# Threshold attention and a leaky-ReLU MLP on one core: four small moves of work between and along the engines' queues

## The chip, the cores and the metric

The kernel runs on one core of a Trainium2 chip. A core has a matrix engine (TensorE, PE in the profile, with its weight loads as PEld), a vector engine (VectorE, DVE), an activation engine (ScalarE, ACT), a general engine (GpSimd, POOL) and a queue for transfers (SyncE, SP). Each engine works through its own instructions in order, and semaphores hold an instruction until what it needs is there. The metric is the time of one execution on the device in microseconds (us); lower is better.

## The reference

Eight batches of eight heads, 576 tokens, 64 elements a head, then an MLP over the 4608 tokens with 512 inputs and 2048 hidden units:

```
scores = q @ k^T / sqrt(64)
scores = where(scores >= max(scores) - tau, scores, -1e9)      # tau = 0.02
attn   = exp(scores - max(scores));  attn /= sum(attn) + 1e-9
x      = (attn @ v), heads side by side                        # [4608, 512]
h      = x @ w_in;  g = max(0.01 * h, h);  out = g @ w_out
```

All inputs and the output are fp32 in memory.

## The kernel before

The work is cut into 144 steps, 18 for each batch. A step is 128 queries of a pair of heads (h = 0, 1); steps go over two blocks of 256 queries, four pairs p and two halves c, and two more steps a batch take the last 64 queries of all heads ("tail" steps). Two steps c = 0, 1 share one tile of weights. The code is written by hand in the order of a loop over n (lines 482 to 522), and each engine's queue has exactly this order: nothing is scheduled later.

What a step n issues, in this order:

- loads for later batches on SP, `loads_at`
- `exps` of step n-1 on ACT: exp of the scores less their largest. In "steep" steps (all before step 12, later those with no turning in the next step) the second head is done with Prelu and Exp on ACT, which need the threshold; otherwise VectorE masks it
- `scores` of step n on PE (L217): three products of fp16 high and low halves of q and k, into PSUM. There is room for one step's scores, so the next ones wait for the score copy
- `copy_min` on DVE (L225, here called the score copy): scaled and negated scores to SBUF, and their minimum `mn` for each head
- `evacuate` of a PV of the step before: x = PV times the widened 1/sum, on DVE (L326; L316 for tails, tile `xt`)
- the first job of `pool_at` on GpSimd, then `threshold` (L232: `th` = `mn` + tau, on DVE for the first 14 steps and on GpSimd from then on), then the other jobs of `pool_at`: splits of q and k into fp16 halves (L138, L144, L148), casts of v (L107, L112), loads of the MLP's weights (L444, L447)
- for step n-1 `weights` on DVE (L264: mask and sum), `recip` (L270: 1/sum) and `widen` (L273: 1/sum copied 64 times into slot 9 of the weights' tile, on GpSimd). In the first 8 steps ("early") recip and widen come after every step, later once for two steps
- the weights are turned: on PE (`turn_w_pe`, L291, in the step after) for the 8 early steps, with the two halves copied back by ACT and DVE (L293); otherwise by a transposing transfer from SP's queue (`turn_w`, L281). The widened 1/sum is turned with them, which is how it comes to lie along the queries
- one unit of `layer1` (L347, L349), if one is ready; the turning of q and k halves on PE (`turn`, L177, copied back at L180 to L188); two half-units of `layer2` (L360), if there are any
- `pv` (L304) of an earlier pair, 4 steps behind (3 for early steps), into the one PSUM buffer `pv`

A group of 256 tokens is complete when the x of its last pair is formed. It then makes 8 units of layer 1, which may start in the step after the one in which x is issued (`l1q`, with `n + 1`), and then 16 half-units of layer 2. Tail tokens of two batches form a group of 128 with 4 and 8. One unit and two half-units a step are what the loop takes.

Before the loop the first pairs are prepared. `split_now` (L151) makes the halves of a pair on ACT (high half, L158) and DVE (low half, L159). For pair 0's k and q, the tail of k, and pair 1's k and q (`first[0]` to `first[4]`) all halves come before step 0; the next ones are split on GpSimd (`split_pool`).

Of the kernel before, what the change touches and what calls it, by code (L numbers as in the profile page):

```python
# [9 lines left out]
FP32 = mybir.dt.float32  # L10
FP16 = mybir.dt.float16
AX = mybir.AluOpType
AF = mybir.ActivationFunctionType
# [25 lines left out]
def kernel(  # L39
# [10 lines left out]
    nc = tc.nc  # L50
# [4 lines left out]
    tau_f = float(tau)  # L55


    UNIT = 64.0 * 64.0 * 8.0
    sb = ctx.enter_context(tc.tile_pool(name="sb", bufs=1))
# [64 lines left out]
    def pair_of(b, p, which):  # L124
        return raws[b, p // 2, which][:, ds(2 * (p % 2), 2), :].rearrange("p h (t d) -> p h t d", d=64)

    def new_half():
        return sb.tile([128, 2, 4, 2, 64], FP16, tag="half", bufs=4, name="half")
# [22 lines left out]
    def split_now(key):  # L151
        t = halves[key] = new_half()
        for i in range(2):
            if key[1] == "t":
                src, n = tails[key[0], key[2]][:, :, i, :], 2
            else:
                src, n = pair_of(*key)[:, i, :, :], 4
            nc.scalar.activation(out=t[:, 0, 0:n, i, :], in_=src, func=AF.Copy, bias=0.0, scale=64.0)  # L158
            nc.vector.scalar_tensor_tensor(out=t[:, 1, 0:n, i, :], in0=src, scalar=64.0, in1=t[:, 0, 0:n, i, :],  # L159
                                           op0=AX.mult, op1=AX.subtract)  # L160
# [58 lines left out]

    def copy_min(st):  # L220

        st.mn = sb.tile([128, 2], FP32, tag="mn", bufs=3, name="mn")
        st.s = sb.tile([128, 2, 576], FP32, tag="s", bufs=2, name="s")
        for h in range(2):
            nc.vector.tensor_scalar(  # L225
                out=st.s[:, h, :].rearrange("p (a b) -> p a b", a=2), in0=st.sc[h][:, :, 0:288],
                scalar1=-1.0 / UNIT, scalar2=None, op0=AX.mult, op1=AX.min, accum_out=st.mn[:, h : h + 1])

    def threshold(st):
        st.th = sb.tile([128, 2], FP32, tag="th", bufs=3, name="th")  # L230
        eng = nc.vector if st.n < 14 else nc.gpsimd
        eng.tensor_scalar(out=st.th[:, :], in0=st.mn[:, :], scalar1=1.0, scalar2=tau_f, op0=AX.mult, op1=AX.add)  # L232

    def exps(st):

        c = 0 if st.tail else st.c
        if c == 0:
            pairs["now"] = pr = Pair()
            pr.w = sb.tile([128, 2, 10, 128], FP16, tag="w", bufs=3, name="w")
            pr.sum = sb.tile([128, 2, 2], FP32, tag="sum", bufs=3, name="sum")  # L240
            pr.n = 1 if st.tail else 2
        st.pair = pr = pairs["now"]
        flat = pr.w[:, c, :, :].rearrange("q n d -> q (n d)")
        st.w = [flat[:, ds(576 * h, 576)] for h in range(2)]
        st.sum = [pr.sum[:, c, h : h + 1] for h in range(2)]
        st.e = sb.tile([128, 2, 576], FP16, tag="e", bufs=2, name="e")
        for h in range(2):
            if h and st.steep:
                z = st.s[:, h, :]
                nc.scalar.activation(out=z, in_=z, func=AF.Prelu, bias=st.th[:, h : h + 1], scale=-1.0, alpha=1e20)  # L250
                nc.scalar.activation(out=st.w[h], in_=z, func=AF.Exp, bias=minus_tau[:, :], scale=1.0,  # L251
                                     accum_out=st.sum[h])
            else:
                nc.scalar.activation(out=st.e[:, h, :], in_=st.s[:, h, :], func=AF.Exp, bias=st.mn[:, h : h + 1],  # L254
                                     scale=-1.0)

    pairs = {}
# [4 lines left out]
    def weights(st):  # L262
        for h in range(1 if st.steep else 2):
            nc.vector.scalar_tensor_tensor(  # L264
                out=st.w[h], in0=st.s[:, h, :], scalar=st.th[:, h : h + 1], in1=st.e[:, h, :],
                op0=AX.is_le, op1=AX.mult, accum_out=st.sum[h])

    def recip(pr, c, n):
        pr.rec = sb.tile([128, 2, 2], FP32, tag="rec", bufs=2, name="rec")
        nc.vector.reciprocal(out=pr.rec[:, 0:n, :], in_=pr.sum[:, ds(c, n), :])  # L270

    def widen(pr, c, n):
        nc.gpsimd.tensor_copy(out=pr.w[:, ds(c, n), 9, :].rearrange("q c (h d) -> q c h d", h=2),  # L273
                              in_=pr.rec[:, 0:n, :].unsqueeze(3).to_broadcast([128, n, 2, 64]))

    def new_wt(pr):
        pr.wt = sb.tile([128, 2, 10, 128], FP16, tag="wT", bufs=4, name="wT")
# [17 lines left out]
    def pv(st):  # L295
        st.pv = ps.tile([128, 4, 128], FP32, tag="pv", bufs=1, name="pv")
        wt = st.pair.wt
        for u in range(2 if st.tail else 1):
            for i in range(5):
                for h in range(2):  # L300
                    blk = i if h == 0 else 9 - i
                    rhs = wt[:, 0, blk - (blk > 4), ds(64 * u, 64)] if st.tail else wt[:, :, blk - (blk > 4), :]
                    o = st.pv[ds(64 * h, 64), 0, ds(64 * u, 64)] if st.tail else st.pv[ds(64 * h, 64), 0:2, :]
                    nc.tensor.matmul(out=o, lhsT=v16[st.b % 2][:, st.p + u, blk, :], rhs=rhs,  # L304
                                     start=(i == 0), stop=(i == 4), skip_group_check=True)
# [3 lines left out]
    def evacuate(st, n):  # L309
        wt = st.pair.wt  # L310
        if st.tail:
            if (st.b % 2, st.c) == (0, 0):
                groups["t"] = xg = Group(128, (st.b, None))
                xg.x = sb.tile([128, NP, 128], FP16, tag="xt", bufs=2, name="xt")
            xg = groups["t"]
            nc.vector.tensor_tensor(  # L316
                out=xg.x[:, ds(st.p, 2), ds(64 * (st.b % 2), 64)],
                in0=st.pv[:, 0, :].rearrange("d (u q) -> d u q", u=2),
                in1=wt[:, 0, 9, :].rearrange("d (u q) -> d u q", u=2), op=AX.mult)
            done = (st.b % 2, st.c) == (1, 1)  # L320
        else:
            if st.p == 0:
                groups["m"] = xg = Group(256, (st.b, 2 * st.blk))
                xg.x = sb.tile([128, NP, 256], FP16, tag="x", bufs=3, name="x")
            xg = groups["m"]
            nc.vector.tensor_tensor(out=xg.x[:, st.p, :].rearrange("d (c q) -> d c q", c=2), in0=st.pv[:, 0:2, :],  # L326
                                    in1=wt[:, :, 9, :], op=AX.mult)
            done = st.p == NP - 1
        if done:
            nu = 8 if xg.tokens == 256 else 4  # L330
            l1q.extend((xg, u, nu, n + 1) for u in range(nu))
# [55 lines left out]
    def units(b):  # L387
        u = [(b, p, w_) for p in range(NP) for w_ in "kq"]
        return u[:2] + [(b, "t", "k")] + u[2:] + [(b, "t", "q")]
# [68 lines left out]
    first = units(0)  # L458
# [2 lines left out]
    turn(first[0])  # L461
    turn(first[1], nc.vector.tensor_copy)
    turn(first[2])
    for key in first[3:5]:
        split_now(key)
    for key in first[5:7]:
        split_pool(key)
    for i in range(4):
# [11 lines left out]
    pv_at = {s.n + PV_LAG - s.early: s for s in steps if s.tail or s.c == 1}  # L480
    n = 0
    while n < N + PV_LAG + 2 or l1q or l2q or stores:
        for f in loads_at.get(n, []):
            f()
        if 1 <= n <= N:
            exps(steps[n - 1])
        if n < N:
            scores(steps[n])
            copy_min(steps[n])
        if n - 1 in pv_at:  # L490
            evacuate(pv_at[n - 1], n)
        todo = pool_at.get(n, [])
        for f in todo[:1]:
            f()
        if n < N:
            threshold(steps[n])
        for f in todo[1:]:
            f()
        if 1 <= n <= N:
            last = steps[n - 1]  # L500
            weights(last)
            if last.early:
                recip(last.pair, last.c, 1)
                widen(last.pair, last.c, 1)
            elif last.tail or last.c == 1:
                recip(last.pair, 0, last.pair.n)
                widen(last.pair, 0, last.pair.n)
                turn_w(last.pair)
        while stores:
            store()  # L510
        if l1q and l1q[0][3] <= n:
            layer1()
        for f in turns_at.get(n, []):
            f()
        if 2 <= n < N + 2 and steps[n - 2].early:
            turn_w_pe(steps[n - 2].pair, steps[n - 2].c)
        for _ in range(2):
            if l2q:
                layer2()
        if n in pv_at:  # L520
            pv(pv_at[n])
        n += 1
# [1 line left out]
_INS = ['q', 'k', 'v', 'tau', 'moe_w_in', 'moe_w_out']  # L524
# [31 lines left out]
```

## Time and profile before

| what | value |
|---|---|
| three runs | 520.55, 522.68, 523.26 us; median 522.68 |
| profiled execution | 523.44 us, of which its span is 521.7 us |
| PE busy | 485.7 us, 93% of the span |
| VectorE busy | 422.7 us, 81% |
| ACT busy | 431.9 us, 83% |
| POOL busy | 331.5 us, 64% |
| chain that ended last | PE 65%, DVE 16%, DMA 7%, ACT 6%, POOL 3% |

The profile is of one execution. Its span begins with the first instruction; what lies around it is the difference of 1.7 us. A share of busy time is a mean over stages with different limits, so the stages are looked at one by one. In a listing of instructions each line has the start, the duration, the engine, the line of the kernel, the operation, the tile written and the tiles read; a bracket at the end gives the idle time of the engine just before and what ended it. Lines of the chain have a start, a duration, and the work that the end of the program hung on at that time.

### The profile page before, as it was taken

What the parts mean: (1) busy time and instruction counts of PE and PEld (TensorE: products, weight loads), DVE (VectorE), ACT (ScalarE), POOL (GpSimd) and SP (SyncE); (2) the same over time, 40 slices, a digit from 0 to 9 for tenths busy, and PEclk for the clock granted to TensorE, in tenths of its full rate; (3) what the DMA queues carried; (4) which work ended last, traced back from release to release, by engine and by line L of the source; (5) the groups of instructions that cost most, each with busy time, mean ns of one, the idle gap of its engine ahead of it and who ended that gap; (6) DMA issues with size and microseconds to landing.
All of it is one profiled execution on the core that took longest, in us unless ns stands there. A gap on an engine that the chain in (4) does not pass through costs nothing.

```text
span 521.7 us, 19307 instructions
## 1 busy us (share of the span) xinstructions
PE 485.7 (93%) x7904; PEld 342.0 (66%) x7904; DVE 422.7 (81%) x1200; ACT 431.9 (83%) x733; POOL 331.5 (64%) x545
## 2 busy tenths in 40 slices
PE   5777887999999999999999999999999999999996
PEld 3454665667767766677666766667666766667773
DVE  4899998999999878988899888988899888888100
ACT  5699896998988978998889888998889889999541
POOL 4956699787777767677667777687667872222000
PEclk9899899999999999999999999999999999999999
DMA  8992975989968998889979988879969975757611
GB/s 244 249 230 48 175 171 112 177 193 203 230 116 172 200 204 177 168 152 231 191 146 182 194 199 188 163 155 233 186 149 184 195 158 135 127 102 151 134 43 62
DMA packets 220697, 87.76 MB, mean 168 GB/s; under 512 B 190912, under 2 KB 217536, under 8 KB 220608
## 3 DMA queue, kind: packets, MB, share of 16 engines
q1 hardware_dynamic: 217648, 82.07, 75.3%
q0 software_dynamic: 2688, 4.19, 4.4%
q8 instruction: 62, 1.02, 0.8%
q14 instruction: 27, 0.22, 0.1%
q10 hardware_dynamic: 272, 0.26, 0.1%
HBM read 36.70 MB, written 9.44 MB: 88 GB/s over the span
## 4 chain that ended last, share of the span: by engine, by line
PE 65%; DVE 16%; DMA 7%; ACT 6%; POOL 3%; issue 2%; DVEq 0%; POOLq 0%
PE hp L347 20%; PE o L360 18%; PE sc L217 17%; DVE s L225 8%; DMA wT<-w 7%; PE pv L304 6%; DVE w L264 5%; PE tp L177 4%; ACT e L254 1%; ACT s L250 1%; DVE x L326 1%; ACT kT L188 1%; DMA raw<-in_k_dram 1%; POOL half L148 1%; ACT osb L366 1%
## 5 line engine op out<-in xcount | busy, mean ns | idle before, releaser
L225 DVE TENSOR_SCALAR_CACHE_REDUCE s<-sc 128x576 f32<-128x576 f32 x288 | 205.2, 750 | 46.0 <-PE sc L217 40.5
L264 DVE SCALAR_TENSOR_TENSOR w<-s,th,e 128x576 f16<-128x576 f32 x210 | 177.2, 866 | 1.9 <-DMA wT<-w 1.7
L254 ACT ACTIVATE e<-s,mn 128x576 f16<-128x576 f32 x210 | 155.7, 774 | 1.5 <-DVE s L225 1.3
L360 PE MATMUL o<-wout,g 128*64 128x512 f16 x1152 | 147.5, 379 | 0.7 <-ACT osb L366 0.7
L217 PE MATMUL sc<-kT,qT 64*128 64x288 f16 (+1 forms) x1920 | 139.8, 290 | 7.8 <-DVE s L225 7.5
L347 PEld LDWEIGHTS <-win 128*64 128x64 f16 x2560 | 118.4, 110 | 33.0 <-issue 30.7
L347 PE MATMUL hp<-x,win 128*64 128x256 f16 x2048 | 136.8, 277 | 0.0
L349 ACT ACTIVATE g<-hp 128x512 f16<-128x512 f32 x144 | 85.1, 591 | 58.8 <-PE hp L347 58.2
L217 PEld LDWEIGHTS <-qT 64*128 64x128 f16 (+1 forms) x1920 | 78.6, 98 | 61.4 <-issue 46.4
L232 POOL TENSOR_SCALAR th<-mn 128x2 f32<-128x2 f32 x130 | 54.9, 422 | 84.4 <-DVE s L225 56.6
L360 PEld LDWEIGHTS <-g 128*64 128x64 f16 x1152 | 62.1, 110 | 31.3 <-issue 1.5
L148 POOL TENSOR_TENSOR half<-scaled,half 128x512 f16<-128x512 f32 (+1 forms) x75 | 81.5, 1087 | 1.7
L144 POOL CAST half<-scaled 128x512 f16<-128x512 f32 (+1 forms) x75 | 62.5, 834 | 4.8 <-POOL th L232 0.2
L273 POOL CAST w<-rec 128x256 f16<-128x256 f32 (+1 forms) x84 | 32.0, 381 | 52.2 <-DVE rec L270 50.0
L304 PE MATMUL pv<-wT,v 128*64 128x256 f16 (+1 forms) x960 | 54.1, 248 | 9.8 <-DMA wT<-w 5.2
L250 ACT ACTIVATE s<-s,th 128x576 f32<-128x576 f32 x78 | 60.3, 773 | 3.4 <-POOL th L232 1.9
L251 ACT ACTIVATE w<-s,minus_tau 128x576 f16<-128x576 f32 x78 | 60.5, 775 | 2.8
L304 PEld LDWEIGHTS <-v 128*64 128x64 f16 x960 | 40.8, 111 | 29.9 <-DMA wT<-w 11.5
L177 PE MATMUL tp<-ident,half 128*64 128x128 f16 x1152 | 49.3, 229 | 7.6 <-ACT half L158 5.2
L138 POOL TENSOR_SCALAR scaled<-raw 128x512 f32<-128x512 f32 x60 | 48.3, 805 | 7.8 <-DMA raw<-in_k_dram 5.9
L177 PEld LDWEIGHTS <-half 128*64 128x64 f16 x1152 | 42.3, 116 | 11.8 <-ACT half L158 5.9
L188 ACT COPY kT<-tp 128x1024 f16<-128x1024 f16 x32 | 32.3, 1008 | 5.6 <-PE tp L177 5.6
(39 smaller groups left out, 278.8 us busy)
## 6 DMA issues: line engine op xcount, KB each, us to landing
vraw<-in_v_dram SPq DMA_DIRECT2D x16, 512.0 KB, 5.1
out_dram<-osb SPq DMA_DIRECT2D x16, 512.0 KB, 3.4
raw<-in_k_dram SPq DMA_DIRECT2D x14, 512.0 KB, 4.7
raw<-in_q_dram SPq DMA_DIRECT2D x14, 512.0 KB, 4.8
win<-in_moe_w_in_dram POOLq DMA_DIRECT2D x4, 512.0 KB, 10.9
wout<-in_moe_w_out_dram POOLq DMA_DIRECT2D x4, 512.0 KB, 9.1
wT<-w SPq DMA_TRANSPOSE x76, 5.2
raw<-in_k_dram SPq DMA_DIRECT2D x4, 256.0 KB, 4.3
```

The lines of the kernel that those rows point to most:

```text
L144: nc.gpsimd.tensor_copy(out=halves[key][:, 0, 0:n, :, :], in_=scaled[key][:, 0:n, :, :])
L148: nc.gpsimd.tensor_tensor(out=halves[key][:, 1, 0:n, :, :], in0=scaled.pop(key)[:, 0:n, :, :], in1=halves[key][:, 0, 0:n, :, :], op=AX.sub ...
L177: nc.tensor.transpose(o, half[:, x, t, h, :], ident[:, :])
L217: nc.tensor.matmul(out=o, lhsT=lhs, rhs=turned[st.b, "k"][rows, kx, pair, ds(key0, 288)], start=(i == 0), stop=(i == 2), skip_group_check= ...
L225: nc.vector.tensor_scalar(out=st.s[:, h, :].rearrange("p (a b) -> p a b", a=2), in0=st.sc[h][:, :, 0:288], scalar1=-1.0 / UNIT, scalar2=No ...
L250: nc.scalar.activation(out=z, in_=z, func=AF.Prelu, bias=st.th[:, h : h + 1], scale=-1.0, alpha=1e20)
L254: nc.scalar.activation(out=st.e[:, h, :], in_=st.s[:, h, :], func=AF.Exp, bias=st.mn[:, h : h + 1], scale=-1.0)
L264: nc.vector.scalar_tensor_tensor(out=st.w[h], in0=st.s[:, h, :], scalar=st.th[:, h : h + 1], in1=st.e[:, h, :], op0=AX.is_le, op1=AX.mult, ...
L304: nc.tensor.matmul(out=o, lhsT=v16[st.b % 2][:, st.p + u, blk, :], rhs=rhs, start=(i == 0), stop=(i == 4), skip_group_check=True)
L347: nc.tensor.matmul(out=hp[ds(64 * u2, 64), jj, :], lhsT=w_in16[:, i, ds(128 * j + 64 * u2, 64)], rhs=g.x[:, i, :], start=(i == 0), stop=(i ...
L349: nc.scalar.activation(out=g.g[:, ds(nj * u, nj), :], in_=hp[:, :, :], func=AF.Prelu, bias=0.0, scale=1.0, alpha=0.01)
L360: nc.tensor.matmul(out=g.o[ds(64 * u2, 64), :], lhsT=g.g[:, j, ds(128 * m + 64 * u2, 64)], rhs=w_out16[:, j, :], start=(j == 0), stop=(j = ...
```

## The change

Four edits:

- `mn` and `th` become [128, 2, 2] in place of [128, 2], and only the first element of each pair is used: the two thresholds of a step lie 8 bytes apart. The instructions are the same.
- `widen` takes an engine, and the 8 early steps give it VectorE. The later ones stay on GpSimd.
- The split of pair 1's q (`first[4]`) is issued in step 0 after the first score copy, no longer before the loop. On DVE its two instructions now stand behind the two of the score copy; the order on ACT and PE stays.
- `evacuate` is called straight after `pv` at the end of the same step, no longer in the next step behind the score copy. On DVE x moves ahead of the next step's score copy. A group becomes ready for layer 1 one step earlier: its first unit is issued in step 11 where it was step 12, and the stores on SP follow a step earlier too.

```diff
     def copy_min(st):
-        st.mn = sb.tile([128, 2], FP32, tag="mn", bufs=3, name="mn")
+        st.mn = sb.tile([128, 2, 2], FP32, tag="mn", bufs=3, name="mn")
...
-                scalar1=-1.0 / UNIT, scalar2=None, op0=AX.mult, op1=AX.min, accum_out=st.mn[:, h : h + 1])
+                scalar1=-1.0 / UNIT, scalar2=None, op0=AX.mult, op1=AX.min, accum_out=st.mn[:, h, 0:1])

     def threshold(st):
-        st.th = sb.tile([128, 2], FP32, tag="th", bufs=3, name="th")
+        st.th = sb.tile([128, 2, 2], FP32, tag="th", bufs=3, name="th")
         eng = nc.vector if st.n < 14 else nc.gpsimd
-        eng.tensor_scalar(out=st.th[:, :], in0=st.mn[:, :], scalar1=1.0, scalar2=tau_f, op0=AX.mult, op1=AX.add)
+        eng.tensor_scalar(out=st.th[:, :, 0], in0=st.mn[:, :, 0], scalar1=1.0, scalar2=tau_f, op0=AX.mult, op1=AX.add)
...
-    def widen(pr, c, n):
-        nc.gpsimd.tensor_copy(out=pr.w[:, ds(c, n), 9, :].rearrange("q c (h d) -> q c h d", h=2),
-                              in_=pr.rec[:, 0:n, :].unsqueeze(3).to_broadcast([128, n, 2, 64]))
+    def widen(pr, c, n, eng=None):
+        (eng or nc.gpsimd).tensor_copy(out=pr.w[:, ds(c, n), 9, :].rearrange("q c (h d) -> q c h d", h=2),
+                                     in_=pr.rec[:, 0:n, :].unsqueeze(3).to_broadcast([128, n, 2, 64]))
...
-    for key in first[3:5]:
-        split_now(key)
+    split_now(first[3])
...
             copy_min(steps[n])
-        if n - 1 in pv_at:
-            evacuate(pv_at[n - 1], n)
+        if n == 0:
+            split_now(first[4])
...
             if last.early:
                 recip(last.pair, last.c, 1)
-                widen(last.pair, last.c, 1)
+                widen(last.pair, last.c, 1, nc.vector)
...
         if n in pv_at:
             pv(pv_at[n])
+            evacuate(pv_at[n], n)
```

More of the change, by code (lines that the diff above doesn't have):

```diff
@@ L249, in exps @@
                 z = st.s[:, h, :]
-                nc.scalar.activation(out=z, in_=z, func=AF.Prelu, bias=st.th[:, h : h + 1], scale=-1.0, alpha=1e20)
+                nc.scalar.activation(out=z, in_=z, func=AF.Prelu, bias=st.th[:, h, 0:1], scale=-1.0, alpha=1e20)
                 nc.scalar.activation(out=st.w[h], in_=z, func=AF.Exp, bias=minus_tau[:, :], scale=1.0,
@@ L253, in exps @@
             else:
-                nc.scalar.activation(out=st.e[:, h, :], in_=st.s[:, h, :], func=AF.Exp, bias=st.mn[:, h : h + 1],
+                nc.scalar.activation(out=st.e[:, h, :], in_=st.s[:, h, :], func=AF.Exp, bias=st.mn[:, h, 0:1],
                                      scale=-1.0)
@@ L264, in weights @@
             nc.vector.scalar_tensor_tensor(
-                out=st.w[h], in0=st.s[:, h, :], scalar=st.th[:, h : h + 1], in1=st.e[:, h, :],
+                out=st.w[h], in0=st.s[:, h, :], scalar=st.th[:, h, 0:1], in1=st.e[:, h, :],
                 op0=AX.is_le, op1=AX.mult, accum_out=st.sum[h])
```

## The prediction

> **What bounds the kernel now.** I read four views in this order: the windows, the waits by engine, the chain of the first 100 us, and the order of time around single steps. First the windows: core time, then busy time of PE, PEld, DVE, ACT and POOL, and the granted clock.
>
> ```profile
> 13.00:26.00 13.00, 9.58 (x122) 6.35 (x123) 10.55 (x28) 9.01 (x16) 12.57 (x20) 0.84 1.11 250
> 39.00:52.00 13.00, 9.13 (x151) 6.16 (x152) 12.54 (x39) 11.86 (x19) 8.65 (x15) 1.00 0.30 50
> 300.00:350.00 50.00, 49.41 (x802) 34.59 (x800) 43.85 (x126) 43.81 (x75) 37.36 (x61) 1.00 0.85 178
> 500.00:510.00 10.00, 10.00 (x204) 7.91 (x201) 0.00 (x0) 4.78 (x8) 0.00 (x0) 1.00 0.14 54
> ```
>
> There are three stages. Up to about 65 us PE is idle for a quarter of the time; from 39 to 52 DVE is busy for 12.54 of 13 us and sets the pace. From 91 to 480 PE is the bound (382.1 of 389.0 us busy). From 480 PE alone finishes the MLP. So a gain on DVE counts only early, and later only what makes PE wait.
>
> The chain of the early part (start, duration, what):
>
> ```profile
> 17.82 1.68 POOL half L148
> 19.50 0.60 POOL scaled L138
> ...
> 20.85 1.67 POOL half L148
> 22.52 0.24 POOL w L273
> 22.77 0.04 issue
> 22.81 0.32 PE wp L291
> ...
> 36.55 0.57 DVE th L232
> 37.12 0.49 DVE w L264 x2
> ```
>
> POOL's splits stand in front of the first widening (L273), and PE's turn of the first weights waits for it; from 31 to 64 the chain is nearly all DVE. What the threshold on DVE waits for is seen by laying POOL beside DVE:
>
> ```profile
> 36.35 0.81 POOL L447 DMA_DIRECT2D wout<-in_moe_w_out_dram  x1
> ```
>
> ```profile
> 36.55 0.57 DVE L232 TENSOR_SCALAR th<-mn 128x2 f32<-128x2 f32 x1
> ```
>
> The threshold takes 0.16 when POOL rests (33.59). Here it ends at 37.12, as POOL's instruction ends (37.16); at 39.89 it ends with POOL's subtraction (40.42). The 14 on DVE average 0.356, so 0.20 of waiting each, at most 0.46.
>
> A steady stretch, PE and then DVE:
>
> ```profile
> 259.85 0.51 PE L304 MATMUL pv<-wT,v 128*64 128x64 f16 x20
> ...
> 263.41 0.51 PE L304 MATMUL pv<-wT,v 128*64 128x64 f16 x20 [0.36 <-DVE xt L316]
> ```
>
> ```profile
> 258.01 0.76 DVE L225 TENSOR_SCALAR_CACHE_REDUCE s<-sc 128x576 f32<-128x576 f32 x1 [0.94 <-PE sc L217]
> ...
> 259.37 0.42 DVE L326 TENSOR_TENSOR x<-pv,wT 128x256 f16<-128x256 f32 x1
> ...
> 263.07 0.28 DVE L316 TENSOR_TENSOR xt<-pv,wT 128x128 f16<-128x128 f32 x1
> ```
>
> DVE stands idle before the score copy of just the step that follows a PV, and x comes only after that copy. Where two PVs follow each other, PE waits for xt, as PV has one PSUM buffer.
>
> The last stage, one loop turn from start to start:
>
> ```profile
> 497.82 1.05 PE L347 MATMUL hp<-x,win 128*64 128x256 f16 x16
> 498.69 1.04 PE L360 MATMUL o<-wout,g 128*64 128x512 f16 x8
> 499.56 1.05 PE L347 MATMUL hp<-x,win 128*64 128x256 f16 x16
> ```
>
> **x at the end of PV's step.** No instruction is added. DVE runs x ahead of the next score copy, POOL's thresholds and SP's order are kept, except that stores come a step earlier. It adds a wait of DVE for PV; behind it stands the score copy, whose scores come behind the same PV on PE anyway. PV ends 0.84 before those scores, and x takes 0.42, so it fits where DVE is idle (52 waits for scores, 38.0 us, between 91 and 480: median near 0.7).
>
> *Tail.* A group becomes ready for layer 1 one step earlier (step 11, not 12). Following the queues through, 130 layer-1 units and 246 half-units of layer 2 stand before the last scores, not 129 and 244: one turn of 1.74 us leaves the end. It goes into step 11 and step 18, where PE is not the bound: in step 11 it was idle 1.00 + 0.40 us for DVE, and a unit takes 0.99 (1.85 at the low clock that 54.06 shows). Bounds there: 1.6 better (the clock stays up through 52.5 to 56) to 0.5 worse; I take 0, as the idle of 1.38 at 62.30 was followed by full speed. **-1.74.**
>
> *Waits of PE.* Five waits for xt (0.36 to 0.39) go: -1.83. The wait of 1.17 for x at 84.01 goes, but the score copy behind x then ends 0.35 later than it did, so -0.55. x no longer stands between the score copy and the weights, so the weights are 0.34 earlier; of PE's waits for the transposed weights (191.06, 249.93, 308.80, 368.01, 427.29: 1.22 to 0.24) that helps where SP was free, three times some 0.3: -0.9. Where DVE is late (115.43), the score copy now comes up to 0.34 later, and a group's first layer-1 unit can wait 0.1 for x: +0.4, bounds 0 and 1.7 (five such). **-2.9.**
>
> **The first 8 widenings on DVE.** POOL loses eight of 0.29; DVE gains eight. Each must await its reciprocal, so about 0.3 (reciprocal 0.17, of which 0.10 was already counted, and 128 elements, between the 0.17 of the reciprocal and the 0.29 of POOL's). It is one source, SBUF to SBUF, like the threshold, so I add the threshold's mean wait of 0.20; c = 0.5, bounds 0.2 (no wait, short) and 2.0 (all of the longest POOL instruction, 1.68).
>
> **Pair 1's q split behind the first score copy.** DVE's first score copy moves from 12.99 to about 11.6, its exp on ACT from 13.78 to 13.3 (the kT copy stands before it). But PE's transposes of that q wait for its low halves, now behind the copy (1.4), and the scores of step 1 stand behind them: ready at 14.4, done at 15.0 instead of waiting for DVE till 14.47. Step 1 is 0.7 later.
>
> **The opening, walked.** With free thresholds and widenings at no cost: score copy 1 at 16.7 (was 15.89), weights 0 at 18.3, turned weights no longer wait the 2.98 till 22.81; now DVE is late next: copy 2 ends 20.8, weights, reciprocal, q copy 0.6 and wT copy 0.4 follow, copy 3 starts at 23.0 (was 24.71), copy 4 at 26.1 (28.33), x and copy 5 end at 31.3 (33.6). Lead 2.3, q's 0.7 included. From there DVE is the chain. Eight widenings cost 8 x 0.5 = 4.0, all on DVE's path.
>
> **Strided thresholds.** The seven that waited sat at 14.46, 17.37, 20.17 (1.07 over 0.17 together, within the walk) and 36.55, 39.89, 52.74, 58.61 (1.56). No row shows a strided pair. Bounds: no wait (-1.56, and the walk stands) or as before (+1.07 on the walk). The DVE row of the same size that never waits is the reciprocal (0.17, 24 times, beside the same POOL work), so the form decides, not the size; a strided pair is another form, and I take no wait. On POOL, from step 14, nothing changes.
>
> Opening: -2.3 + 4.0 - 1.56 = **+0.1**. Sum: 0.1 - 2.9 - 1.74 = -4.5. The profiled execution (523.44, span 521.7) is 0.76 above the median; from it 518.9, from the median of 522.68 **518.2**.
>
> The Trainium skill, "SBUF — State Buffer", Who interferes with whom, says that VectorE in a two-port mode and GpSimd exclude each other for whole instructions; the two ends above agree. Its "Vector Engine (DVE) Microarchitecture Reference", 5.1, asks for SBUF operands and an even outermost dimension, and for no unit step: by that the strided pair would wait as before, and the sum be rival B's.
>
> **The rivals.**
> - A, neither waits: stepped operands keep both the strided threshold and the widening (its source repeats) clear of POOL, c = 0.3. Opening -2.3 + 2.4 - 1.56 = -1.5; 516.6. For it: the reciprocal's rows. Against: the widening writes densely.
> - B, the stride does nothing: opening -2.3 + 1.07 + 4.0 = +2.8; sum -1.9, 520.8. For it: stride or not, the same two elements move.
> - C, slower: x delays the score copy. Place: 91 to 480, each second step, price 0.34 where DVE comes late; all 64 would be 21.8. It cancels the gain of 4.5 at 13 exposed steps, and is 0.5% slower at 21: with 30, 522.7 + 5.7 = 528.4. Against it: DVE idles in 52 of some 58 such steps.
> - D, the widening meets POOL's long subtractions (1.09 mean): c near 1.0 gives opening +4.1, 522.2. POOL is busy 71% of 13 to 65, but mostly with shorter instructions.
>
> **How the numbers follow.** Forecast 0.35, A 0.24, B 0.23, C 0.08, D 0.10. 0.5% is 2.6 us, about what can be told from no change. The forecast, A and a third of B lie under 520.1: 0.66; the rest of B and D within: 0.25; C above 525.3 and a little else: 0.09. The range goes from A with the kept clock and no late copies (516.6 - 1.6 - 0.4 = 514.6) to D with all five late copies (522.2 + 1.3 = 523.5); C is left out.
>
> **What would show it.** Right: x directly before the score copy, no PE wait for xt, 1.74 less after the last PV; no PE wait for the widening near 20; thresholds at 0.17. Wrong: DVE thresholds still ending with POOL's instructions (B), widenings of 1 us (D), more waits of scores for score copies past 91 (C). A copy 5 ending later than 33.6 would break the walk.

## The result, and the profile after

| | before | after |
|---|---|---|
| runs | 520.55 to 524.66 us, median 522.97 (4 runs) | 516.40 to 517.84 us, median 517.16 (4 runs) |
| profiled execution (span) | 523.44 us (521.7) | 517.33 us (515.6) |
| PE / VectorE / ACT / POOL busy | 485.7 / 422.7 / 431.9 / 331.5 us | 482.9 / 432.6 / 431.8 / 339.8 us |

The ratio is 0.9892, 95% interval 0.985 to 0.9934: faster by 1.1%. A second set of runs of the same kernel gave 517.15 us and 0.9877 (0.9852 to 0.9903).

To see where the time went I laid the two executions beside each other by steps, taking the start of each step's score copy (L225), and cut them into three stretches:

| stretch | before | after | difference | forecast |
|---|---|---|---|---|
| start to the score copy of step 48 | 172.00 | 173.75 | +1.75 | -0.44 |
| step 48 to step 143 (the last) | 308.28 | 301.56 | -6.72 | -2.34 |
| step 143 to the end of the span | 41.4 | 40.3 | -1.1 | -1.74 |
| span | 521.7 | 515.6 | -6.1 | -4.5 |

(In the forecast column the terms of the prediction are put where they act: the opening's +0.1, the wait at 144.82, the one at 84.01 and the late copies in the first row; four waits for xt and the transposed weights in the second.) The sum came near; each of its three parts did not. The first row compares two single executions, and the granted clock differs between them: the kernel before had PE at 0.50 from 21.8 to 28.6 us and from 52.5 to 55.9, the change only from 63.5 to 66.9. Each execution kept here shows one to four such stretches of some 3.4 us between 21 and 126 us, at other places each time.

The middle stretch in the windows of the kernel before (core time, then busy time of PE, PEld, DVE, ACT, POOL, the granted clock, DMA share, GB/s):

```profile
172.00:480.28 308.28, 303.38 (x5012) 212.02 (x5014) 266.34 (x766) 271.75 (x464) 199.89 (x332) 1.00 0.85 175
```

and of the changed kernel:

```profile
173.75:475.31 301.56, 301.36 (x4994) 213.43 (x4996) 271.91 (x766) 271.85 (x464) 209.26 (x333) 1.00 0.89 177
```

PE's idle time there falls from 4.90 us to 0.20: no wait of PE of any size is left there. The waits that are gone, in the waits of PE of the kernel before between 140 and 480 us (us in total, times, longest):

```profile
PE pv L304 <- DMA wT<-w: 1.9, 3, 1.2
PE pv L304 <- DVE xt L316: 1.8, 5, 0.4
PE pv L304 <- DVE w L264: 1.6, 2, 0.8
```

In the changed kernel this view is empty. From step 48 on these are four waits for xt (1.44) and, once a batch, the wait for the transposed weights of its fourteenth step (second block, third pair; 191.06 to 427.29: 1.22 + 0.44 + 0.24 + 0.79 + 0.76 = 3.45), together 4.89. The other 2.02 us of the 6.72 lie in PE's busy time: 16 matmuls less in the stretch up to step 60 (0.46), and 1.56 without any other work gone. Successive groups of matmuls overlap in the records (a layer-1 unit of 1.06 us starts its successor after 0.90), and at a wait this overlap of 0.16 is missing; nine waits make 1.4. By that a wait of PE cost about its idle time and 0.16 more. This is an accounting from the records; no run isolates it. Nor is all of the 6.72 the change's: the run of one-element thresholds alone, further down, has the same code as the kernel before from step 14 on, and its middle stretch took 306.69 us, 1.59 less, with waits for transposed weights of 2.2 us in place of 3.45. Nine executions of kernels with x moved and nothing held back lie between 301.1 and 301.7. So by these profiles the gain there is 5.0 to 7.1 us.

A batch's tail steps in the changed kernel, PE and then DVE:

```profile
259.19 0.48 PE L304 MATMUL pv<-wT,v 128*64 128x64 f16 x20
...
260.44 1.06 PE L347 MATMUL hp<-x,win 128*64 128x256 f16 x16
261.34 1.03 PE L360 MATMUL o<-wout,g 128*64 128x512 f16 x8
262.20 0.48 PE L304 MATMUL pv<-wT,v 128*64 128x64 f16 x20
```

```profile
256.48 0.42 DVE L326 TENSOR_TENSOR x<-pv,wT 128x256 f16<-128x256 f32 x1 [0.23 <-PE pv L304]
257.39 0.76 DVE L225 TENSOR_SCALAR_CACHE_REDUCE s<-sc 128x576 f32<-128x576 f32 x1 [0.49 <-PE sc L217]
...
260.44 0.28 DVE L316 TENSOR_TENSOR xt<-pv,wT 128x128 f16<-128x128 f32 x1
260.63 0.75 DVE L225 TENSOR_SCALAR_CACHE_REDUCE s<-sc 128x576 f32<-128x576 f32 x1
```

x now sits in the idle time ahead of the score copy, which still waits 0.49 for its scores after it, and the second PV finds its buffer free.

The opening is another matter. The first thresholds of the changed kernel on DVE, and what POOL did beside them:

```profile
18.50 0.53 DVE L232 TENSOR_SCALAR th<-mn 128x2 f32<-128x2 f32 x1
...
53.37 0.50 DVE L232 TENSOR_SCALAR th<-mn 128x2 f32<-128x2 f32 x1
...
58.77 0.81 DVE L232 TENSOR_SCALAR th<-mn 128x2 f32<-128x2 f32 x1
```

```profile
17.84 1.15 POOL L148 TENSOR_TENSOR half<-scaled,half 128x512 f16<-128x512 f32 x1
...
53.23 0.62 POOL L138 TENSOR_SCALAR scaled<-raw 128x512 f32<-128x512 f32 x1
...
58.39 1.16 POOL L148 TENSOR_TENSOR half<-scaled,half 128x512 f16<-128x512 f32 x1
```

Each long one ends with POOL's instruction (19.03 and 18.99, 53.87 and 53.85, 59.58 and 59.55). The stride takes no wait away: six of the 14 thresholds still take 0.23 to 0.81. In all they take 4.40 us, before 4.99; POOL did other work beside them, and the run of dense thresholds below separates the two. The widenings on DVE:

```profile
L273 DVE CAST w<-rec x8: 226/233/440, 20.5 to 45.1; 128x128 f16<-128x128 f32 x8
```

(min, median and max in ns.) Two of the eight took 0.44 and 0.30 and ended within 0.09 of the end of a POOL instruction, the others took 0.23 to 0.24. From the start of the reciprocal to the start of what follows the widening it is 3.06 us for the eight; less the prediction's 0.10 for each reciprocal (0.08 to 0.10 before), the eight add 2.26 us to DVE, 0.28 each.

The q split behind the first copy shows on PE in the changed kernel:

```profile
11.79 1.06 PE L177 MATMUL tp<-ident,half 128*64 128x128 f16 x15 [0.33 <-DVE half L159]
14.46 0.97 PE L177 MATMUL tp<-ident,half 128*64 128x128 f16 x8 [1.61 <-DVE half L159]
```

Score copy 0 is 1.33 earlier (11.66), score copy 1 is 1.13 later (17.02 for 15.89), score copy 2 is 1.97 later. PE's wait of 2.98 for the widening at 22.81 is gone, and score copy 3 is back at the time before (-0.07). There the opening stays: copy 5 starts 0.39 later, although PE ran at half its clock in steps 3 and 4 of the kernel before and not in those of the change.

### The profile page after: what moved, and what is told of

Its sections match the earlier page's. It is cut to its first block, busy times and chain, and to the rows that moved or that the text cites. A ratio compares the mean times of both kernels' runs of the same rounds, so it can differ in the third digit from the quotient of the medians.

```text
span 515.6 us, 19350 instructions
## 1 busy us (share of the span) xinstructions
PE 482.9 (94%) x7904; PEld 343.9 (67%) x7904; DVE 432.6 (84%) x1208; ACT 431.8 (84%) x733; POOL 339.8 (66%) x537
## 4 chain that ended last, share of the span: by engine, by line
PE 72%; DVE 12%; DMA 6%; ACT 6%; issue 2%; POOL 1%; SPq 0%; DVEq 0%; POOLq 0%; ACTq 0%
PE hp L347 22%; PE o L360 21%; PE sc L217 18%; PE pv L304 6%; DMA wT<-w 6%; DVE s L225 5%; PE tp L177 4%; DVE w L264 4%; ACT e L254 2%; ACT s L250 1%; DMA rawt<-in_k_dram 1%; ACT w L251 1%; ACT g L349 1%; DVE th L232 1%; DVE wT L293 1%
## 5 line engine op out<-in xcount | busy, mean ns | idle before, releaser
L225 DVE TENSOR_SCALAR_CACHE_REDUCE s<-sc 128x576 f32<-128x576 f32 x288 | 206.1, 753 | 27.5 <-PE sc L217 24.8
L264 DVE SCALAR_TENSOR_TENSOR w<-s,th,e 128x576 f16<-128x576 f32 x210 | 178.9, 875 | 1.1 <-POOL th L232 0.8
L232 POOL TENSOR_SCALAR th<-mn 128x2 f32<-128x2 f32 x130 | 80.8, 622 | 88.1 <-DVE s L225 63.9
L304 PEld LDWEIGHTS <-v 128*64 128x64 f16 x960 | 43.2, 111 | 19.6 <-issue 5.3
L144 POOL CAST half<-scaled 128x512 f16<-128x512 f32 (+1 forms) x75 | 50.7, 676 | 7.6 <-PE tp L177 3.0
L273 POOL CAST w<-rec 128x256 f16<-128x256 f32 (+1 forms) x76 | 29.1, 383 | 30.9 <-DVE rec L270 28.7
```

Of the source, the lines that this page charges most:

```text
L225: nc.vector.tensor_scalar(out=st.s[:, h, :].rearrange("p (a b) -> p a b", a=2), in0=st.sc[h][:, :, 0:288], scalar1=-1.0 / UNIT, scalar2=No ...
L232: eng.tensor_scalar(out=st.th[:, :, 0], in0=st.mn[:, :, 0], scalar1=1.0, scalar2=tau_f, op0=AX.mult, op1=AX.add)
L264: nc.vector.scalar_tensor_tensor(out=st.w[h], in0=st.s[:, h, :], scalar=st.th[:, h, 0:1], in1=st.e[:, h, :], op0=AX.is_le, op1=AX.mult, ac ...
```

## The experiments

All times are medians of four to twelve executions, of which one gave the profile; the kernel before ran on the same chip. Its medians were 523.23 us for the first four runs, 523.52 for the next four and 523.25 for the last four. A ratio's interval is about plus or minus 0.0027, so two of these kernels are told apart from some 2 us on; where a difference is smaller I say what the traces show. The granted clock goes with the times: of the runs of x alone the fastest had a mean of 0.995 (516.28 us), the slowest 0.982 (518.93), by which I estimate 0.2 us for each 0.001. The means of two kernels differ by up to 0.006 (without x last), so differences near 1 us can be the clock's.

### The parts of the change

**x alone.** The kernel before, with x formed at the end of PV's step:

```diff
-        if n - 1 in pv_at:
-            evacuate(pv_at[n - 1], n)
...
             pv(pv_at[n])
+            evacuate(pv_at[n], n)
```

> Only x is moved to the end of PV's step; the three edits of the opening are left as before. Theory 1 (the gain is x's: the PE waits for xt and for the transposed weights once a batch, and one loop turn at the end; the three opening edits together bring nothing): 516 to 518 us, step 143's score copy 4 to 6 us earlier than before. Theory 2 (the sum on record: x's own steps bring 4.6, the opening nothing net): 518.3. Rival (the opening edits bring a third or more of the gain): above 519.

517.72 us, ratio 0.989 (0.9862 to 0.9918). This is the whole of the change's gain within what can be told: step 48 to 143 takes 301.63 us (301.56 in the change), the end is 1.29 shorter.

**Dense thresholds.** The change with its thresholds dense again:

```diff
-        st.th = sb.tile([128, 2, 2], FP32, tag="th", bufs=3, name="th")
+        st.th = sb.tile([128, 2], FP32, tag="th", bufs=3, name="th")
...
-        eng.tensor_scalar(out=st.th[:, :, 0], in0=st.mn[:, :, 0], scalar1=1.0, scalar2=tau_f, op0=AX.mult, op1=AX.add)
+        eng.tensor_scalar(out=st.th[:, :], in0=st.mn[:, :], scalar1=1.0, scalar2=tau_f, op0=AX.mult, op1=AX.add)
```

> The changed kernel with the thresholds dense again ([128, 2]), all else kept. Theory 1 (a strided threshold waits for POOL as a dense one does; the waits became rarer because POOL no longer waits for the widening and runs ahead): within 0.5 us of the changed kernel, the 14 thresholds on DVE again between 0.17 and 0.8 us, each long one ending with an instruction of POOL. The forecast's step (the stride takes the wait away): 1.6 to 2.6 us slower than the changed kernel, with long thresholds where the changed kernel has short ones.

517.12 us, ratio 0.9876 (0.9849 to 0.9902), and the thresholds in order of time are those of the strided kernel, 0.3 us earlier:

```profile
53.05 0.50 DVE L232 TENSOR_SCALAR th<-mn 128x2 f32<-128x2 f32 x1
...
58.45 0.81 DVE L232 TENSOR_SCALAR th<-mn 128x2 f32<-128x2 f32 x1
```

All 14 take 4.39 us, with the stride 4.40. The stride does nothing to the wait.

**Widenings back on GpSimd**, the rest of the change kept:

```diff
-                widen(last.pair, last.c, 1, nc.vector)
+                widen(last.pair, last.c, 1)
```

> The changed kernel with the first 8 widenings on GpSimd again. Theory 1: PE waits again about 3 us for the first widening near 20 us, DVE is spared 8 x 0.28 = 2.3 us, POOL is chained to DVE again; score copy 9 within 1 us of the changed kernel's, total within 1 us. Rival (the widening's move is what helps the opening): 2 us slower or more.

516.78 us, ratio 0.9867 (0.9841 to 0.9894): not to be told from the change. PE's wait for POOL's widening is back, and costs nothing that can be told in the end:

```profile
23.08 0.32 PE L291 MATMUL wp<-ident,w 128*64 128x128 f16 x2 [2.85 <-POOL w L273]
```

**q split before the first copy**, the rest of the change kept:

```diff
-    split_now(first[3])
+    for key in first[3:5]:
+        split_now(key)
...
-        if n == 0:
-            split_now(first[4])
```

> The changed kernel with pair 1's q split ahead of the first score copy again. Theory 1 (the split behind the copy only delays PE's turn of that q and with it the scores of step 1): score copy 1 starts 0.7 to 1.1 us earlier than in the changed kernel, total 0 to 1 us faster. Rival (the earlier first copy and its exp are worth something): slower by 0.5 us or more.

517.11 us, ratio 0.9874 (0.9846 to 0.9901): the change's time to 0.1 us, though score copy 1 is 2.2 us earlier than in the change. In its trace PV waits 4.4 us for transposed weights before 84 us (in the change about 1.0; two more waits of 1.1 follow at 96 and 134): much of the lead of the first steps is given back there.

**The change once more**, nothing edited, for the opening:

> The changed kernel itself once more, on the same chip as the three others, for what two profiles of one program differ by in the first 170 us. Score copy 36 came 2.3 us later than before in its first profile, and 0.3 later with x alone. Theory 1 (the opening edits bring nothing, and the difference is the arrival of transfers): within 1 us of x alone in time, and a score copy 36 between 0 and 2.3 us later than before.

517.15 us, ratio 0.9877 (0.9852 to 0.9903). Score copy 36 starts 2.03 later than in the kernel before and score copy 48 2.14 (2.30 and 1.75 in the first profile): in both of its profiles the opening is behind that of the one profile of the kernel before.

### Why moving x brings so much

**Layer 1 late.** x moved, but layer 1 may start only where it did:

```diff
-            l1q.extend((xg, u, nu, n + 1) for u in range(nu))
+            l1q.extend((xg, u, nu, n + 2) for u in range(nu))
...
-        if n - 1 in pv_at:
-            evacuate(pv_at[n - 1], n)
...
             pv(pv_at[n])
+            evacuate(pv_at[n], n)
```

> Only x moved, as in the run of x alone, but a group's layer 1 may start one step later, so in the same step as before the change. It tells the loop turn at the end from the waits of PE. Theory 1 (two separate gains): the steps from 172 us on pull ahead as with x alone, about 1.1 to 1.3 us a batch, but the end is one turn (1.74 us) longer: 1.0 to 1.8 us slower than x alone, 518.7 to 519.5 us, and no PE wait of layer 1 for x. Rival (the earlier layer 1 is itself what takes the waits away): the waits of PV for the transposed weights stay, 521 us or more.

519.07 us, ratio 0.9929 (0.9905 to 0.9953). Its middle stretch takes 304.11 us, 4.2 less than before where x alone has 6.65 less, and the waits of PE between 140 and 480 us are

```profile
PE pv L304 <- DMA wT<-w: 2.3, 3, 1.4
```

So x's own place removes the waits for xt. That it shortens those for transposed weights is not shown: 2.3 us are left of 3.45, but one-element thresholds alone, with x unmoved, has 2.2. They go away together with the earlier layer 1: in nine executions that have it, with the stores as they follow from it, 0.4 us or less is left from step 48 on. The time is that of theory 1, the reason is in part the rival's.

What follows an earlier layer 1 on SP is that the stores of finished groups come earlier. SP's queue in the kernel before, up to the transfer that the wait at 191.06 is for, the last line:

```profile
171.98 0.58 SPq L375 DMA_DIRECT2D out_dram<-osb  x1
...
175.29 4.95 SPq L281 DMA_TRANSPOSE wT<-w  x1
...
181.59 1.60 SPq L93 DMA_DIRECT2D vraw<-in_v_dram  x1
183.30 4.18 SPq L281 DMA_TRANSPOSE wT<-w  x1
```

and in x alone, where the store went out at 166.85:

```profile
176.15 3.41 SPq L281 DMA_TRANSPOSE wT<-w  x1
...
182.68 4.11 SPq L281 DMA_TRANSPOSE wT<-w  x1
```

The kernel with the late layer 1 has the store where the kernel before has it (170.14, and 4.97 for the first of the two transfers). In the kernel before the queue is in use until 183.19, so the awaited transfer starts 0.93 after its weights are complete (182.37); in x alone it starts 0.03 after (182.65), and PV waits 0.15 in place of 1.22. That is one batch of five. In the other four the awaited transfer of the kernel before starts 0.02 to 0.35 after its weights, and PV waits 0.24 to 0.79. The weights themselves may count too: from the start of their score copy they take 7.6 us before and 7.3 with x moved. And in the kernel with the late layer 1 the transfer of the first batch shown starts 1.06 after its weights, and PV does not wait for it at all. So neither the store nor the weights is shown to be the cause alone.

**x last.** The kernel before with x behind the weights, the reciprocal and the issue of the transposes, to take x out of the weights' way without moving layer 1:

```diff
-        if n - 1 in pv_at:
-            evacuate(pv_at[n - 1], n)
...
+        if n - 1 in pv_at:
+            evacuate(pv_at[n - 1], n)
```

> The kernel before with x put behind the weights, the reciprocal and the issue of the transposing transfer of its step, so later than before. The weights come 0.34 us earlier as in the change, but x and xt come about 1.5 to 2 us later. Theory 1 (PV's waits for the transposed weights went because the weights are earlier): PE's waits for the transfer between 140 and 480 us shrink to under 1.5 us from 3.5 (five), while its waits for xt grow from 0.36 to 1.5 or more each: 523 to 530 us in all. Rival (it is the early x, not the early weights, that ends those waits): PE's waits for the transfer stay at 3 us or more.

540.67 us, ratio 1.033 (1.0302 to 1.0358): far slower than either theory had it. As PV has one buffer, x itself is now late; the waits of PE between 140 and 480 us:

```profile
PE pv L304 <- DVE x L326: 10.0, 6, 2.2
PE pv L304 <- DVE xt L316: 3.7, 6, 0.6
PE pv L304 <- DMA wT<-w: 1.9, 4, 0.9
```

On the transposed weights it decides nothing (1.9 us lies between the two bounds), since PV's times are others here; it shows the price of the opposite move.

**Stores late.** x moved and layer 1 early, but each store is held back one turn of the loop:

```diff
-                stores.append(g)
+                held.append(g)
...
+        stores.extend(held)
+        held.clear()
```

(with x moved as above)

> x at the end of PV's own step, as in the run of that part alone, but each store of an output group is issued one loop turn later, the turn in which the kernel before issues it. Theory (moving x moves the stores, and so takes them from ahead of the transposing transfers of the tail steps on SP; that is why PV's waits for DMA go): between 140 and 480 us PV waits again some 2 us for DMA-transposed weights, and the time is 1 to 2.5 us above the 517.7 of x alone (518.7 to 520). Rival (the stores' place does not matter, layer 1's earlier place or x's own place does it): no DMA wait of PV in that stretch, and within 0.5 us of x alone (517.2 to 518.2).

519.18 us, ratio 0.9919 (0.9888 to 0.995): inside the theory's 518.7 to 520, 1.46 above x alone, which is within the two intervals. Its profiled run is the fastest of its six (517.18); in it the middle stretch takes 303.11 us, 1.5 more than x alone, and PV waits again, but for less than the 2 us expected:

```profile
PE pv L304 <- DMA wT<-w: 1.1, 3, 0.5
```

So the stores' place seems to make a part of these waits: 303.11 us lies outside the 301.1 to 301.7 of the nine executions with early stores. That is one execution, and where PV waits for transfers one and the same code has differed by 1.59 us, so the size, 1.5 of the 2.5 us that the earlier layer 1 brings in this stretch, is not settled; the medians point the same way and do not separate it. What makes the other 1.0 (of which 0.46 are the 16 matmuls) is left open.

### What would have freed the thresholds

**One element at a time.** x moved, and each of the first 14 thresholds as two instructions of one element:

```diff
-        eng.tensor_scalar(out=st.th[:, :], in0=st.mn[:, :], scalar1=1.0, scalar2=tau_f, op0=AX.mult, op1=AX.add)
+        for h in range(2):
+            if st.n < 14:
+                nc.vector.tensor_scalar(out=st.th[:, h : h + 1], in0=st.mn[:, h : h + 1], scalar1=1.0, scalar2=tau_f,
+                                        op0=AX.mult, op1=AX.add)
+            elif h == 0:
+                nc.gpsimd.tensor_scalar(out=st.th[:, :], in0=st.mn[:, :], scalar1=1.0, scalar2=tau_f, op0=AX.mult, op1=AX.add)
```

> Only x moved, and each threshold of the first 14 steps on DVE split into two instructions of one element each. If what makes a threshold wait for POOL is that it is read and written in two halves at once, an instruction of one element has no second half and never waits: 28 thresholds of 0.17 us or less, the sum of waits 2.1 us gone, 14 more instructions at about 0.08; score copy 14 1 to 1.5 us earlier than with x alone, total 0 to 1.5 us faster. If any such instruction waits for POOL: still up to 0.8 us each.

514.89 us, ratio 0.9839 (0.9813 to 0.9865), 2.8 us below x alone and more than the 0 to 1.5 expected; the intervals just touch. None of the 28 waits (count, busy us, mean ns, idle before):

```profile
L234 DVE TENSOR_SCALAR th<-mn 128x1 f32<-128x1 f32 x28 | 3.8, 150 | 0.0
```

A pair takes 0.27, where a threshold of two elements took 0.17 to 0.81; score copy 14 starts 2.46 earlier than in the kernel before (x alone: 0.39 later), and the lead stays. Not all of that is the edit's: 1.65 of it is there at copy 5, where layer 1 late and stores late, with two elements, are 1.48 and 1.21 ahead as well. From step 5 to step 14 it gains 0.81 where these two and x alone lose 0.42 to 0.47, so 1.2 to 1.3 us can be put down to the thresholds. The form does not touch the weights (L264), which wait for POOL too: they take 0.81 to 0.82 where POOL rests and up to 1.33 beside it here, in the first 14 steps 2.2 us of waiting, in x alone 2.0.

**The same alone.** The kernel before, x unmoved, with this edit:

> The kernel before with one thing changed: each of the first 14 thresholds as two one-element instructions. Theory (the one-element form never waits for GpSimd; two of them cost 0.30 us where a waiting pair cost 0.36 on average, and those on the chain 0.5 to 0.8): 1.5 to 3 us faster than before (520.2 to 521.8), as the same edit beside x moved gave 2.8. Rival (it pays only where x is out of the way): within 0.7 us of before.

521.88 us, ratio 0.9985 (0.9961 to 1.0009), 12 runs. The theory's lower price and the rival's 0.7 both miss it: 1.4 below before, not told from no change by the times. In its profiled run (its fastest, 520.11) score copy 14 starts 2.86 earlier and step 48 still 2.11, like beside x moved. The other 1.59 come in the middle stretch, where no code differs, and the end takes 0.38 more. The times of twelve runs bear out less than half of that run's 3.3.

**With the widenings on VectorE**, x moved and one-element thresholds:

> x at the end of PV's step, the first 14 thresholds as two one-element instructions each, and the first 8 widenings on VectorE; q split and strides as in the kernel before. Theory (a widening costs DVE 0.28 us and frees the turned weights from a PE wait of some 3 us near 20 us, but from then on DVE is the chain to 65 us): 8 x 0.28 = 2.3 us of DVE against what the wait costs; the same prices with dense thresholds gave 0.35 us against the move, so 514.5 to 516, against 514.9 with the widenings on GpSimd. Rival (once the thresholds cost nothing, PE's wait near 20 us is what is left of the opening): 512 to 513.5.

514.87 us, ratio 0.9851 (0.9819 to 0.9883), with them on GpSimd 514.89. Inside the theory's 514.5 to 516: once more the place of the widenings makes no difference that can be told. That DVE pays what PE gains near 20 us is the theory's account; no run isolates it.

**Widening first.** x moved, one-element thresholds, the widenings on GpSimd, and there ahead of the splits of their step in steps 1 and 2:

```diff
-        for f in todo[:1]:
+        behind = 1 <= n <= 2
+        for f in todo[:1] if not behind else []:
             f()
...
+        if behind:
+            for f in todo:
+                f()
```

> x at the end of PV's step and one-element thresholds as above, the widenings on GpSimd as in the kernel before, but GpSimd's splits of steps 1 and 2 are placed behind the widening of their step instead of ahead of it. Theory (PE's wait of some 3 us for the first widening comes only from GpSimd's queue, which has two splits ahead of it): that wait goes without any work added to DVE, and 0 to 2 us of it last to the end: 513 to 515 against 514.9. Rival (the splits then come late and PE waits for their transposes instead, or DVE is the chain there anyway): 514.9 to 516.5.

513.12 us, ratio 0.9808 (0.9776 to 0.984): the best of all, 10.1 us below before and 1.8 below the same without this move, though these two intervals overlap. The wait of 2.87 at 22.27 has become one of 0.81:

```profile
20.11 0.25 PE L296 MATMUL wp<-ident,w 128*64 128x128 f16 x2 [0.81 <-POOL w L278]
```

Score copy 3 starts 2.87 earlier than in the kernel before (1.32 without the move), but step 48 only 1.16 (2.26 without), so in the two profiles the lead of the first steps is gone by 65 us; the gain in the medians is not explained by them. The profiled execution is the slowest of its six (514.31), that without the move the fastest of its five (513.21).

Two of the stretches of the main kernels side by side, from one profile each (us from step 48 to step 143, against 308.28 before):

| kernel | median | step 48 starts | step 48 to 143 |
|---|---|---|---|
| change | 517.16 | +1.75 | 301.56 |
| x alone | 517.72 | +0.62 | 301.63 |
| x moved, layer 1 late | 519.07 | -1.94 | 304.11 |
| x moved, stores late | 519.18 | +0.13 | 303.11 |
| x moved, one-element thresholds | 514.89 | -2.26 | 301.57 |
| the same, widening first | 513.12 | -1.16 | 301.52 |
| one-element thresholds alone | 521.88 | -2.11 | 306.69 |

## Why the prediction was right, and where its steps were wrong

518.2 was forecast, faster; it is 517.16. Against the profiled execution's 518.9 the sum is 1.6 too high. The sign was carried by one part, x, as the run of x alone shows, and for the reason given: DVE idles where x now stands. That the size came out so near was luck: errors of 2.2 and 0.6 us one way and 4.4 the other.

- **The waits for xt, -1.83: right.** All five are gone, and the score copy is not delayed: rival C fell. In the changed kernel no score copy between 140 and 480 makes PE wait.
- **The transposed weights, -0.9: too small, and not only by its own mechanism.** The weights did come 0.33 earlier. But all 3.45 us of waits went, and only with the earlier layer 1; with layer 1 late 2.3 us stayed. The prediction noted that the stores come a step earlier, and priced nothing for it; with the stores held back the stretch took 1.5 us more. Nor was the overlap of matmuls counted that a wait takes from PE (about 1.4, by the accounting above). This is the largest error, -6.72 for -2.34; up to 1.6 of it can be scatter, as one and the same code differed by 1.59 here.
- **The tail, -1.74: the turn is gone, net -1.1 to -1.3.** Between the last PV and the end PE has one turn less; 0.2 us more of waits for ACT's `osb` and 0.2 for x take some of it back.
- **The turn's new place at 0: not borne out.** The prediction put it into step 11 and 18 and took its cost as nothing, bounds 1.6 better to 0.5 worse. From step 5 to step 48 x alone, stores late and the change fall back by 0.65, 1.34 and 1.36 us; with late layer 1 it is 0.46 ahead. By these the turn costs 1.1 to 1.8 there, about what it saves at the end, but the other executions with early layer 1 run from 0.61 ahead to 3.16 behind, so no size is settled. Where something is lost can be seen: all ten executions with early layer 1 have PE waiting for the transposed weights of steps 19, 31 or 33, between 84 and 141 us, 1.0 to 2.4 us in all (the change: 1.10 at 96.45 and 1.12 at 134.28). The four with late layer 1, the kernel before among them, have no such wait there. The prediction has no term for this. Against this the earlier layer 1 brings 2.5 us in the middle stretch by the profiles; over the whole time the medians of x alone and layer 1 late differ by 1.4 (not separated).
- **The strided thresholds, -1.56: the step that fell.** "A strided pair is another form, and I take no wait": it waits like the dense one, to 0.01 us. Rival B had the mechanism right, and its 520.8 only missed as the middle stretch gave so much more. The Trainium skill, "Vector Engine (DVE) Microarchitecture Reference", 5.1, asks for an outermost dimension that is even, or odd and of one size in source and destination, and for no unit step; by that the stride could not help, and the run agrees (4.40 for 4.39 us). What a single element does is told by the run alone: 28 instructions at 0.15.
- **The widening, c = 0.5: measured 0.28.** The bound of 2.0 was not come near: the longest widening on DVE in any run is 0.79 (20.28, q split before). Its waits (0.21 at 27.39, 0.07 at 38.25) show that the copy does wait as the threshold does, so rival A's "neither waits" is wrong in both halves, though its c of 0.3 is right.
- **The walk, lead 2.3 at copy 5: not there.** It wanted x and copy 5 to end at 31.3; copy 5 alone ends at 33.7. q's split cost step 1 1.13 and step 2 1.97, not 0.7, thresholds in it waited as before (0.71 at 14.66, 0.53 at 18.50), and the widenings came on top. "A copy 5 ending later than 33.6 would break the walk" - it did. But the runs with the widening on GpSimd and with q before show nothing of this that lasts: both end at the change's time.

The three kernels x alone, layer 1 late and stores late are the same program up to step 5, and there their score copies 5 start 0.03, 1.48 and 1.21 us earlier than in the kernel before. The granted clock was low at different places in them (from 24.7, 32.5 and 24.0 us), but x alone is 1.0 behind the other two already at score copy 3, before any of that. So a single profile says nothing of the opening below 1.5 us, and a walk of it to 0.1 us, as the prediction made, promised more than a profile can bear out.

## What to carry to other kernels

When an operation is moved, follow what its being earlier releases, on every queue: here layer-1 units and stores came forward with x, in places that no line of the diff touches, and they decided how large the gain was. Work that leaves the end goes somewhere, and is priced there. And a short instruction that waits for another engine is tested by changing its form, one run for each form: a stride did nothing, one element instead of two made every wait of the thresholds vanish, and left those of the weights.

## What the runs showed of the hardware

- A DVE `tensor_scalar` of 128x2 fp32 beside POOL's work took 0.15 to 1.11 us, with stride 2 as with stride 1. In the ten executions with this form 64 of 140 took over 0.20, and 62 of these ended within 0.04 us of the end of a POOL instruction. Of 128x1 it took 0.14 to 0.16 in all 112 cases of four executions. The Trainium skill, "SBUF — State Buffer", Who interferes with whom, says that VectorE's two-port modes and GpSimd exclude each other for a whole instruction: the ends agree.
- A DVE copy of 128x128 whose source repeats each element 64 times also waited: up to 0.79 where it took 0.23 otherwise, in ten of the 40 cases of five executions.
- DVE's masking of the weights (128x576, scores and exponentials from SBUF) took 0.81 to 0.82 in the 19 cases of the kernel before with no POOL instruction beside it, and up to 1.57 with one.
- With a store of 512 KB on SP's queue ahead of the loads, the transposing transfer behind them took longer: in the change, the kernel before, x alone, layer 1 late and stores late, at the twelfth step of five batches, 3.74 to 5.16 us on the queue with a store there (13 cases, median 4.57), 3.21 to 3.91 without (12 cases, median 3.4). These are not the transfers that PE waited for; those come next on the queue.
- By the accounting above, an estimate, a wait of PE costs some 0.16 us of the overlap between matmul groups besides the idle time shown.
